# Where the first layer's sums lie, and at which steps W2's halving and the overflow's count are issued

## The chip, the cores and the metric

The kernel runs on one core of a Trainium2 chip. The metric is the time of one execution on the device, in microseconds (us). Five engines work beside one another, each with its own queue, which it takes strictly in order: TensorE (PE, with PEld for its weight loads), VectorE (DVE), ScalarE (ACT), GpSimd (POOL) and SyncE (SP), which here only issues transfers. [...]

## The reference

Attention with a decay, and behind it a layer of eight experts, of which each token uses one. Only the second part matters here. For a token with expert e:

```
logits = x @ w_gate                      # 8 experts
e = argmax(logits), or the expert of the token before it, where a local gate says so
p = softmax(logits)
h = max(x @ w1[e], 0)                    # 512 -> 1024
out = p[e] * (h @ w2[e])                 # 1024 -> 512
```

There are 8 x 576 tokens; all inputs and the output are float32.

## The kernel before

**Precision.** Every float32 operand of a matmul is cut into an upper half (float16) and a lower half (float16, what the upper one leaves out), and each product is made of three: upper with upper, lower with upper, upper with lower. An upper half is written by ScalarE (a copy to float16, L2118, for W2's blocks), a lower one by VectorE, which subtracts the upper half from the scaled value (L2120). A lower half reads two operands: the float32 block and the upper half.

**Stages.** Up to some 458 us the kernel does the attention and the routing. Then come experts 0 and 1 ("fixed", with a part of their tokens done earlier), and from 508 us on the other six, taken by the number of their tokens ("ranks" 0 to 5, with 608, 592, 576, 576, 544 and 480 places). After them stands a loop for tokens that overflow these places; the overflow's count tells how often it runs.

**A fixed expert** (`experts`): the first layer, 8 column blocks of 12 products with 256 or 320 columns into PSUM tiles `z` (two buffers, L1763), each followed by ScalarE's relu (upper half `hh`, L1737) and VectorE's lower half `hl` (L1738). Then the second layer, token tile by token tile, 24 products of 512 columns each into PSUM tiles `y` (two buffers, L1805), which ScalarE scales into SBUF (L1748) and GpSimd scatters to the output (L1750).

**A ranked expert**: the first layer goes through `seven`, which makes a 2 x 2 block product with seven products instead of eight, in 4 groups `g`. A product is 6 matmuls (L1848) of n columns, n being half the rank's places (304, 296, 288, 288, 272, 240). The seven products go into three banks: product 2 into `yt` (G.a); 1, 6, 7 and 4 accumulate in `zb` (G.b); 5 and 3 accumulate in `zd` (G.d). In between, ScalarE copies the state of `zb` to SBUF after products 1, 6 and 7 (`kept`, L1855, tiles `et`). After products 2, 7 and 3, VectorE adds a kept copy to the bank of PSUM (L1861); the sum goes to another tile `et` in SBUF. `finish` then makes `hh` of the sum by ScalarE (L1865) and `hl` by VectorE (L1866), which reads the sum and `hh`. After product 4 there is no add, and `hh` and `hl` read `zb` itself. `finish` of a sum is issued one product later. Product 3 accumulates on `zd` after the add of product 7 has read it.

The order of the products is 1, 2, 4, 6, 3, 5, 7, where 4 and 3 belong to the group before; the last group goes 1, 2, 4, 6, 5, 7, 3 and then its own 4 and 3. Each product is a step; there are 28 in the first layer, numbers 0 to 27. In the last group, steps 19 to 27, product 6 is step 22, 5 is 23, 7 is 24, the other group's 3 is 25, then 4 (26) and 3 (27). The second layer adds some 20 steps. With 592 or 608 places, the second of its token tiles is the one with the rest of the tokens; in rank 5 that tile is the first.

**Work beside the products.** The rest of the work is a list of pairs (step, function): `run` issues a function after the given step's instructions, to the queues of its engines. A step is thus a place in the queues, not a time. In each rank, beside the products:

- `M.second(j, c, low)`: the halves of the rank's own W2, in blocks j = 0 to 3, c = 0 or 1. Block 0 is cut in the rank before (step `UB`), blocks 1 to 3 here at the steps of `UC`: a pair (upper, lower) for each of the six half blocks.
- `N.load`: SP's transfers of the next rank's weights, 512 KB each, into buffers `stg`. Four are issued at step 0, three at the steps of `UN`, and each of those three takes the buffer that a block of `M` has left.
- `XA`: at step 4, GpSimd's gathers of the next rank's tokens (L1695); at step 20, SP's transposes of them (L1700).
- `LA`: at steps 6 to 13, eight operations of GpSimd (`sums`, L2132, L2136, L2141 twice, for c = 0 and 1): sums and differences of the next rank's W1 blocks, 512 columns each, all in SBUF.
- From step 28 on, the token sums (`sums_of`) and the halves of W1 of the next rank (L2098).

Rank 5 has no next rank, so only `M.second` is left there. In fixed expert 0 GpSimd's sums for rank 0 are issued at steps 9 to 16 (`FA`), and `OV[1]`, the overflow's count (`tiles`, from L2409 on, nine small VectorE operations and a memset), at step 13. Its first layer has 16 steps, 0 to 15.

Of the kernel before, what the change touches and what calls it, by code (L numbers as in the profile page):

```python
# [10 lines left out]
F32 = mybir.dt.float32  # L11
# [87 lines left out]
SEVEN = (1, 1, 1, 1, 1, 1)  # L99
WP = (28, 30, 32, 36)  # L100
LA = (6, 7, 8, 9), (10, 11, 12, 13)
UC = (0, 1), (2, 3), (8, 10), (15, 17), (22, 23), (26, 27)
UB = 45
UN = (5, 18, 28)
XA = (4, 20)
WC = (28, 29, 29, 30, 31, 31, 38, 38)
TA = (28, 36, 37, 44)
# [9 lines left out]
def kernel(  # L117
# [14 lines left out]
    DM = H * D  # L132
# [1696 lines left out]
    def seven(W, xT, sums, n, hh, hl):  # L1829

        (bh, bl, ah, al), (th, tl) = W[0:4], sums
        half = slice(0, n), slice(n, 2 * n)

        def given(d, h):
            return lambda c: (xT[:, 2 * d + c, half[h]], xT[:, 4 + 2 * d + c, half[h]])

        def summed(d, h):
            return lambda c: (th[:, c, d, half[h]], tl[:, c, d, half[h]])

        prods = {1: (ah[:, 0], al[:, 0], given(0, 0)), 2: (bh[:, 0], bl[:, 0], given(1, 0)), 3: (bh[:, 2], bl[:, 2], given(1, 1)),  # L1840
                 4: (bh[:, 1], bl[:, 1], summed(1, 0)), 5: (ah[:, 1], al[:, 1], summed(0, 0)),
                 6: (ah[:, 2], al[:, 2], summed(1, 1)), 7: (bh[:, 3], bl[:, 3], summed(0, 1))}

        def mul(p, g, out, start):
            hi, lo, x = prods[p]
            ops = [(w[:, c, g * 128:(g + 1) * 128], v) for c in range(2) for w, v in zip((hi, hi, lo), (*x(c), x(c)[0]))]
            for i, (w, v) in enumerate(ops):
                nc.tensor.matmul(out, lhsT=w, rhs=v, start=(start and i == 0), stop=(i == len(ops) - 1), skip_group_check=True)  # L1848

        def temp():  # L1850
            return EX["fx"].tile([128, 304], F32, name="et", bufs=5)[:, 0:n]

        def kept(x):
            t = temp()
            nc.scalar.copy(t, x)  # L1855
            return t

        def out(fc, h, x, plus=None):
            if plus is not None:
                t = temp()  # L1860
                nc.vector.tensor_tensor(t, x, plus, ALU.add)  # L1861
                x = t

            def finish():
                nc.scalar.activation(hh[:, fc, half[h]], x, AF.Relu)  # L1865
                nc.vector.scalar_tensor_tensor(hl[:, fc, half[h]], x, 0.0, hh[:, fc, half[h]], ALU.max, ALU.subtract)  # L1866

            if plus is None:
                finish()
            else:  # L1870
                later.append(finish)

        later = []

        def do(p, G):
            if p == 1:
                G.b, G.d = (products(1).tile([128, 512], F32, name=x)[:, 0:n] for x in ("zb", "zd"))
            if p == 2:
                G.a = ps3_.tile([128, DM], F32, name="yt")[:, 0:n]
            bank_of = G.a if p == 2 else G.d if p in (3, 5) else G.b  # L1880
            mul(p, G.g, bank_of, p in (1, 2, 5))
            if p in (1, 6, 7):
                G.kept[p] = kept(G.b)
            if p == 2:
                out(G.g, 0, G.a, G.kept[1])
            elif p == 4:
                out(4 + G.g, 0, G.b)
            elif p == 7:
                out(4 + G.g, 1, G.d, G.kept[7])
            elif p == 3:  # L1890
                out(G.g, 1, G.d, G.kept[6])
            while len(later) > (p in (2, 3, 7)):
                later.pop(0)()

        old = None
        for g in range(4):
            G = types.SimpleNamespace(g=g, kept={})
            own, last = ((1, 2, 4, 6, 5, 7, 3), (4, 3)) if g == 3 else ((1, 2, 4, 6, 3, 5, 7), ())
            for p in own:
                x = old if p in (3, 4) else G  # L1900
                if x:
                    do(p, x)
                    yield
            old = G
        for p in last:
            do(p, old)
            if p == last[-1]:
                for f in later:
                    f()
            yield  # L1910
# [104 lines left out]
    ps2_ = ctx.enter_context(tc.tile_pool(name="ps2_", bufs=2, space=PSUM, side="right"))  # L2015
# [3 lines left out]
    def products(kind):  # L2019
        if PZ.get("kind") != kind:  # L2020
            if PZ:
                PZ["stack"].close()
            PZ["kind"], PZ["stack"] = kind, ExitStack()
            PZ["pool"] = PZ["stack"].enter_context(tc.tile_pool(name="psz%d" % len(PZ), bufs=2, space=PSUM))
        return PZ["pool"]
# [180 lines left out]
    def both(*fs):  # L2206
        return lambda: [whole(f) for f in fs]
# [4 lines left out]
    todo = [turn_xl, both(last[0]), both(last[1]), both(*last[2:], close_attention, crit[0]), both(crit[1]), both(crit[2]), both(*crit[3:6]), both(*crit[6:8]), both(*crit[8:10]),  # L2212
            both(*crit[10:13]), both(*crit[13:16]), both(crit[16]), both(*crit[17:19], all_idx, late_tok)]
# [269 lines left out]
    OV = overflow()  # L2483
# [18 lines left out]
    def call(x, f, *args):  # L2502
        return x, lambda: f(*args)
# [7 lines left out]
    def tokens_of(r):  # L2511
        xn = xp_.tile([128, 8, 608], F16, name="xT")
        return xn, *token_steps(xp_, xn, lambda i: T.ranki[:, 0, r, i:i + 1], RANKC[r], bufs=XG)

    N = EX["N"]
    todo = [(8, half_rows), (13, OV[1])]
    todo += [(x, f) for x, f in zip(FA[0], [f for c in C2 for f in N.sums(c)])]
    todo += [(FA[1][0], lambda: N.room(True))]
    todo += [call(FA[1][2 * i + c], f, c) for i, f in enumerate((N.second_row, N.differences)) for c in C2]
# [6 lines left out]
    todo = [call(FA[2][2 * i + c], f, c) for i, f in enumerate((N.first_row, N.total)) for c in C2]  # L2526
# [3 lines left out]
    for r in range(NR):  # L2530
        M, xc, todo = N, xn, []
        todo += [call(y, M.second, (i + 2) // 2, i % 2, low) for i, x in enumerate(UC) for low, y in enumerate(x)]
        if r + 1 < NR:
            N = Halves(lambda r=r: number(r + 1))
            N.x = None
            xn, gs, ts = tokens_of(r + 1)
            todo += [call(0, N.load, ST)] + [call(x, N.load) for x in UN]
            todo += [(XA[0], both(*gs)), (XA[1], both(*ts))]
# [10 lines left out]
        if not SEVEN[r]:  # L2549
            todo = [(x - 12 if x > 27 else x * 16 // 28, f) for x, f in todo]  # L2550
# [89 lines left out]
```

## Time and profile before

| what | us |
|---|---|
| median of 3 runs | 794.24 (793.62 to 799.51) |
| the profiled execution | 788.54 |
| its span | 786.6 |
| TensorE busy | 736.1 (94%) |
| VectorE busy | 613.7 (78%) |
| ScalarE busy | 509.9 (65%) |
| GpSimd busy | 474.8 (60%) |

Rows of the timeline give start, duration, engine, line, operation, out<-in, shape and count; a bracket holds the idle time of the engine ahead of the row and what ended it. TensorE's matmuls are pipelined: a row lasts longer than the distance to the next one's start. The mean granted clock of TensorE over the span is 0.989.

### The profile page before, as it was taken

The numbers are of one execution on the slowest core, as the hardware profiler recorded it, in microseconds if no ns is written. First come the engines' busy times: TensorE is split into PE (matmuls) and PEld (weight loads), VectorE is DVE, ScalarE is ACT, GpSimd is POOL, SyncE is SP. The second block draws the span as 40 slices with busy tenths as digits, with TensorE's granted clock in tenths as the row PEclk, the third lists the DMA queues.
The fourth block names the chain that finished last, engine by engine and source line by source line (L and its number), as shares of the span: only waits on it lengthen the run. The fifth ranks groups of instructions, "written<-read, shape, count | busy, mean of one in ns | idle before, by whom it ended". The sixth has DMA issues, their size and how long they took to land.

```text
span 786.6 us, 21919 instructions
## 1 busy us (share of the span) xinstructions
PE 736.1 (94%) x8661; PEld 535.4 (68%) x8661; DVE 613.7 (78%) x1295; ACT 509.9 (65%) x1006; POOL 474.8 (60%) x521
## 2 busy tenths in 40 slices
PE   5898999999999998989799989999999999998996
PEld 3686888887878877878555565675665657475682
DVE  7786888898898989899758865678687896878650
ACT  7796788988878978868533225456564555657451
POOL 5879969395879859838682474191552838264201
PEclk9999999999999999999999999999999999999999
DMA  7569869788786968155794746274753716664201
GB/s 177 134 129 208 179 151 184 171 147 208 148 193 129 179 146 154 38 108 187 177 266 163 231 115 153 71 242 82 261 124 143 216 67 242 134 234 114 82 2 50
DMA packets 189659, 120.75 MB, mean 154 GB/s; under 512 B 129397, under 2 KB 165511, under 8 KB 189532
## 3 DMA queue, kind: packets, MB, share of 16 engines
q1 hardware_dynamic: 183473, 100.19, 54.1%
q0 software_dynamic: 6080, 19.13, 7.2%
q8 instruction: 69, 1.13, 0.6%
q14 instruction: 37, 0.30, 0.1%
HBM read 72.25 MB, written 19.32 MB: 116 GB/s over the span
## 4 chain that ended last, share of the span: by engine, by line
PE 54%; DVE 15%; issue 12%; POOL 8%; ACT 7%; POOLq 2%; DMA 0%; SPq 0%; ACTq 0%; DVEq 0%
PE y L1805 15%; PE pt L940 8%; PE st L894 6%; PE z L1763 6%; PE xp L919 5%; PE zb L1848 4%; DVE nm L905 3%; DVE pl L949 3%; PE st L429 2%; POOLq L1749 2%; ACT ph L945 2%; ACT P L925 2%; PE zd L1848 2%; DVE hl L1866 1%; POOL s L2141 1%
## 5 line engine op out<-in xcount | busy, mean ns | idle before, releaser
L925 ACT ACTIVATE P<-st,nm 128x512 f32<-128x512 f32 (+3 forms) x288 | 153.0, 588 | 28.0 <-DVE nm L905 23.4
L945 ACT CAST ph<-pt 128x512 f16<-128x512 f32 (+1 forms) x200 | 115.4, 588 | 35.8 <-PE pt L940 33.5
L905 DVE TENSOR_REDUCE nm<-st 128x1 f32<-128x512 f32 (+4 forms) x264 | 133.4, 542 | 6.4 <-PE st L901 3.9
L949 DVE TENSOR_TENSOR pl<-pt,ph 128x512 f16<-128x512 f32 (+1 forms) x165 | 109.2, 670 | 22.9 <-ACT ph L945 20.9
L940 PE MATMUL pt<-ident,P 128*128 128x128 f32 x784 | 121.3, 280 | 5.0 <-DVE pl L949 2.4
L1750 POOL DMA_INDIRECT out_dram<-o,ranki x26 | 34.4, 1323 | 134.7 <-ACT o L1748 102.6
L940 PEld LDWEIGHTS pt<-ident,P 128*128 128x128 f32 x784 | 84.1, 142 | 21.6 <-DVE pl L949 3.7
L919 PE MATMUL xp<-VH,pl 128*128 128x65 f16 (+1 forms) x960 | 89.2, 194 | 6.0 <-DVE pl L949 5.3
L919 PE MATMUL xp<-VH,ph 128*128 128x65 f16 (+1 forms) x960 | 90.6, 195 | 2.0 <-ACT ph L945 2.0
L1805 PEld LDWEIGHTS <-hh 128*128 128x128 f16 x528 | 51.3, 98 | 58.5
L919 PE MATMUL xp<-VL,ph 128*128 128x65 f16 (+1 forms) x960 | 90.1, 194 | 0.0
L919 PEld LDWEIGHTS <-ph 128*128 128x128 f16 (+1 forms) x1920 | 82.9, 102 | 10.3 <-issue 3.0
L894 PE MATMUL st<-Ak,Aq 128*128 128x256 f16 (+4 forms) x448 | 77.7, 284 | 4.6 <-ACT P L925 2.6
L919 PEld LDWEIGHTS <-pl 128*128 128x128 f16 (+1 forms) x960 | 74.7, 102 | 7.2 <-DVE pl L949 6.3
L894 PE MATMUL st<-KB,QB 70*128 70x256 f16 (+4 forms) x448 | 77.4, 281 | 1.9 <-DMA KB<-Ak 1.9
L1805 PE MATMUL y<-uh,hh 128*128 128x512 f16 x168 | 63.7, 379 | 0.0
L1805 PE MATMUL y<-ul,hh 128*128 128x512 f16 x168 | 63.7, 379 | 0.0
L1805 PE MATMUL y<-uh,hl 128*128 128x512 f16 x168 | 63.7, 379 | 0.0
L1763 PE MATMUL z<-xT,wh 128*128 128x384 f16 (+2 forms) x256 | 55.1, 306 | 3.4 <-DVE hl L1738 3.2
L1866 DVE SCALAR_TENSOR_TENSOR hl<-et,hh 128x288 f16<-128x288 f32 (+4 forms) x72 | 40.0, 555 | 23.3 <-ACT hh L1865 21.6
L1865 ACT ACTIVATE hh<-et 128x288 f16<-128x288 f32 (+4 forms) x72 | 31.4, 436 | 30.0 <-DVE et L1861 29.7
L1848 PEld LDWEIGHTS <-wh 128*128 128x128 f16 x384 | 37.5, 98 | 18.2 <-issue 9.8
(436 smaller groups left out, 2000.9 us busy)
## 6 DMA issues: line engine op xcount, KB each, us to landing
stg<-in_moe_w_dram SPq DMA_DIRECT2D x64, 512.0 KB
xs<-xr SPq DMA_DIRECT2D x16, 512.0 KB
ldq<-in_q_dram SPq DMA_DIRECT2D x14, 512.0 KB
ldk<-in_k_dram SPq DMA_DIRECT2D x14, 512.0 KB
ldv<-in_v_dram SPq DMA_DIRECT2D x28, 256.0 KB
QB<-Aq SPq DMA_DIRECT2D x15, 256.0 KB
KB<-Ak SPq DMA_DIRECT2D x15, 256.0 KB
ldv<-in_v_dram SPq DMA_DIRECT2D x20, 64.0 KB
```

The source lines that it names most:

```text
L894: nc.tensor.matmul(st[p0:p0 + m, co:co + n], lhsT=queries(lq, kk, h, c), rhs=rhs, start=(ps == 0 and first and co == col), stop=(ps == 1), ...
L905: nc.vector.tensor_reduce(dst, src, axis=AX.X, op=ALU.max, negate=True)
L919: nc.tensor.matmul(xo, lhsT=a[:, c0:c0 + m], rhs=w[:, vi, :], start=False, stop=(i == n - 1 and jj == 2), skip_group_check=True)
L925: nc.scalar.activation(P[:, c0:c1].rearrange("p (k x r) -> p k r x", r=2, x=64), st[:, c0:c1].rearrange("p (k r x) -> p k r x", r=2, x=64) ...
L940: nc.tensor.matmul(U["pt"][:, i * 128:(i + 1) * 128], lhsT=P[:, i * 128:(i + 1) * 128], rhs=ident, is_transpose=True, start=(i == 0), stop ...
L945: nc.scalar.copy(U["ph"][:, :cols], U["pt"][:, :cols])
L949: nc.vector.tensor_tensor(U["pl"][:, :cols], U["pt"][:, :cols], U["ph"][:, :cols], ALU.subtract)
L1750: nc.gpsimd.indirect_dma_start(out=outf if EX.get("over") else next_out(), out_offset=bass.IndirectOffsetOnAxis(ap=scat(t)[0:m], axis=0), ...
L1763: nc.tensor.matmul(z[:, a, 0:wd], lhsT=w[:, d, fc * 128:(fc + 1) * 128], rhs=xT[:, x, a * wd:(a + 1) * wd], start=(i == 0), stop=(i == len ...
L1805: nc.tensor.matmul(y[0:m], lhsT=a[:, fc, t * 128:t * 128 + m], rhs=u[:, fc], start=(i == 0), stop=(i == len(prods) - 1))
L1848: nc.tensor.matmul(out, lhsT=w, rhs=v, start=(start and i == 0), stop=(i == len(ops) - 1), skip_group_check=True)
L1866: nc.vector.scalar_tensor_tensor(hl[:, fc, half[h]], x, 0.0, hh[:, fc, half[h]], ALU.max, ALU.subtract)
```

## The change

The sum of a kept copy and a PSUM bank (`out`) is written in place into that bank, and after product 7, whose bank `zd` is still to be accumulated on, into a new PSUM tile `y` of the second layer's pool. `UC` and `UN` put the halving of W2's blocks 2 and 3 and two of the three loads at other steps. The overflow's count goes from step 13 to step 19 of fixed expert 0, which is in its second layer.

```diff
-UC = (0, 1), (2, 3), (8, 10), (15, 17), (22, 23), (26, 27)
+UC = (0, 1), (2, 3), (4, 5), (22, 23), (24, 25), (26, 27)
 UB = 45
-UN = (5, 18, 28)
+UN = (5, 24, 29)
...
-        def out(fc, h, x, plus=None):
+        def out(fc, h, x, plus=None, more=False):
             if plus is not None:
-                t = temp()
+                t = ps2_.tile([128, DM], F32, name="y")[:, 0:n] if more else x
                 nc.vector.tensor_tensor(t, x, plus, ALU.add)
                 x = t
...
             elif p == 7:
-                out(4 + G.g, 1, G.d, G.kept[7])
+                out(4 + G.g, 1, G.d, G.kept[7], True)
...
-    todo = [(8, half_rows), (13, OV[1])]
+    todo = [(8, half_rows), (19, OV[1])]
```

## Rows read from the trace of the kernel before

**Rows 1.** The page, busy time of TensorE: us (share of the span) xinstructions.
```profile
PE 736.1 (94%) x8661; PEld 535.4 (68%) x8661; DVE 613.7 (78%) x1295; ACT 509.9 (65%) x1006; POOL 474.8 (60%) x521
```

**Rows 2.** Waits of PE, 508 to 760 us: us in total, times, longest.
```profile
PE zb L1848 <- ACT et L1855: 7.8, 7, 1.6
PE zd L1848 <- DVE et L1861: 0.2, 1, 0.2
```

**Rows 3.** Busy time by windows: first layers of ranks 0, 4, 5; second of 1.
```profile
core 0: us, PE busy (x) PEld busy (x) DVE busy (x) ACT busy (x) POOL busy (x), PEclk, DMA share, GB/s
...
508.30:531.40 23.10, 22.12 (x171) 16.50 (x170) 16.68 (x30) 13.69 (x33) 19.63 (x15) 1.00 0.77 252
...
579.20:603.70 24.50, 24.50 (x198) 13.23 (x196) 20.86 (x26) 14.07 (x20) 7.18 (x5) 1.00 0.34 74
...
696.10:718.50 22.40, 19.98 (x171) 16.45 (x170) 16.56 (x30) 12.92 (x33) 17.12 (x13) 1.00 0.73 247
...
742.00:759.80 17.80, 17.80 (x182) 16.91 (x181) 12.77 (x31) 13.02 (x34) 0.93 (x1) 1.00 0.05 15
```

**Rows 4.** Timeline of rank 0's first layer, 519 to 529 us: start, us, engine.
```profile
519.17 1.28 POOL L2132 TENSOR_TENSOR stg<-stg 128x512 f32<-128x512 f32 x1
...
519.41 1.38 DVE L1866 SCALAR_TENSOR_TENSOR hl<-et,hh 128x304 f16<-128x304 f32 x1 [0.60 <-ACT hh L1865]
...
523.64 1.76 DVE L2120 SCALAR_TENSOR_TENSOR wl<-stg,wh 128x512 f16<-128x512 f32 x1
...
526.68 0.29 PE L1848 MATMUL zd<-tl,uh 128*128 128x304 f16 x1
...
526.81 0.29 PE L1848 MATMUL zd<-th,ul 128*128 128x304 f16 x1
...
527.64 0.39 ACT L1855 COPY et<-zb 128x304 f32<-128x304 f32 x1
...
527.93 0.63 ACT L2118 ACTIVATE wh<-stg 128x512 f16<-128x512 f32 x1
...
528.09 0.29 PE L1848 MATMUL zb<-th,wh 128*128 128x304 f16 x1 [0.98 <-ACT et L1855]
```

**Rows 5.** Lines L1866 and L1861: form, count, ns min/median/max, first and last start.
```profile
L1866 DVE SCALAR_TENSOR_TENSOR hl<-et,hh x72: 400/467/1491, 511.7 to 760.8; 128x288 f16<-128x288 f32 x24, 128x304 f16<-128x304 f32 x12, 128x296 f16<-128x296 f32 x12, 128x272 f16<-128x272 f32 x12
L1866 DVE SCALAR_TENSOR_TENSOR hl<-zb,hh x24: 407/446/474, 515.2 to 759.3; 128x288 f16<-128x288 f32 x8, 128x304 f16<-128x304 f32 x4, 128x296 f16<-128x296 f32 x4, 128x272 f16<-128x272 f32 x4
...
L1861 DVE TENSOR_TENSOR et<-zd,et x48: 399/445/475, 512.9 to 759.9; 128x288 f32<-128x288 f32 x16, 128x304 f32<-128x304 f32 x8, 128x296 f32<-128x296 f32 x8, 128x272 f32<-128x272 f32 x8
```

**Rows 6.** Timeline of rank 5, VectorE, and TensorE's first tile of its second layer.
```profile
757.32 0.69 DVE L2120 SCALAR_TENSOR_TENSOR ul<-stg,uh 128x512 f16<-128x512 f32 x1 [0.39 <-ACT uh L2118]
...
760.81 0.41 DVE L1866 SCALAR_TENSOR_TENSOR hl<-et,hh 128x240 f16<-128x240 f32 x1 [0.47 <-ACT hh L1865]
...
761.27 0.33 PE L1800 MATMUL y<-hl,uh 128*128 128x96 f16 x4
```

**Rows 7.** Timeline of fixed expert 0, 465 to 484 us, VectorE, GpSimd and TensorE.
```profile
465.65 1.20 DVE L2410 TENSOR_SCALAR nov<-nov 128x8 f32<-128x8 f32 x1
...
469.68 0.75 DVE L1738 SCALAR_TENSOR_TENSOR hl<-z,hh 128x256 f16<-128x256 f32 x2
...
483.68 1.23 DVE L2098 SCALAR_TENSOR_TENSOR ul<-stg,uh 128x1024 f16<-128x1024 f32 x1 [5.98 <-ACT uh L2097]
...
466.78 1.27 POOL L2132 TENSOR_TENSOR stg<-stg 128x512 f32<-128x512 f32 x1
...
469.48 2.51 POOL L2141 TENSOR_TENSOR s<-stg,s 128x512 f32<-128x512 f32 x2
...
470.14 0.27 PE L1763 MATMUL z<-xT,wh 128*128 128x256 f16 x1 [2.25 <-DVE hl L1738]
```

**Rows 8.** Timeline of VectorE behind rank 0's first layer, and at rank 1's start.
```profile
536.16 1.39 DVE L1920 TENSOR_TENSOR sx<-xT 128x1184 f32<-128x1184 f16 x1 [1.96 <-DMA xT<-xg]
...
558.22 0.47 DVE L1861 TENSOR_TENSOR et<-yt,et 128x296 f32<-128x296 f32 x1 [3.78 <-PE yt L1848]
```

## The prediction

> **What bounds the kernel now.** I read the page first: TensorE is busy 94% of the span [rows 1], so only its idle time can be won, and I looked for that in the part that the change touches: from fixed expert 0 (458 us) to the first layer of the last ranked expert (760 us). The table by windows shows where it is. The first layers of ranks 0 and 4 have TensorE idle for 1.0 and 2.4 us; that of rank 5, the only one beside which GpSimd makes no weight sums, has none (17.80 busy of 17.80) [rows 3]. The second layers have none either (24.50 of 24.50 in one, and likewise in the others). The list of waits says for what: 7.8 us in 7 waits for the copy of zb (ScalarE, L1855) and 0.2 in one for an add [rows 2].
>
> These numbers are a little short. Inside a stream two matmuls of 304 columns start 0.13 us apart while each row lasts 0.29, so the idle time of each stop is counted 0.16 us short [rows 4]. With 8 stops the loss is 8.0 + 8 x 0.16 = 9.3 us.
>
> Why the copy is late is in the timeline of rank 0 [rows 4]. GpSimd starts its first sum at 519.17. VectorE's hl (L1866) of 519.41 takes 1.38 us and the W2 lower half (L2120) of 523.64 takes 1.76, where the line view has medians of 0.467 for hl, and an L2120 with GpSimd idle takes 0.69 [rows 5, 6]. VectorE falls behind, ScalarE stands behind VectorE's add in its own queue, its copy starts only at 527.64, and TensorE starts product 7 of the last group at 528.09 after 0.98 us of idling.
>
> The line view shows which instructions GpSimd holds up. hl with x in SBUF (et) spreads from 0.400 to 1.491; hl with x in PSUM (zb) never exceeds 0.474, and the adds, with one operand in PSUM, never 0.475 [rows 5]. Both live through the same sums. So what is held up has two operands in SBUF; one with an operand in PSUM is not.
>
> Fixed expert 0 has the same trouble in another form. The overflow's count is issued at step 13, inside sums; its small `nov` operation over 8 columns takes 1.20 us, the hl behind it comes at 469.68, and TensorE waits for it until 470.14, 2.25 us, the larger of 2 such waits [rows 7].
>
> **The change part by part.**
>
> *Sums in PSUM.* 12 adds per rank, 72 in all, write PSUM instead of SBUF, and the 72 relu and 72 hl behind them read PSUM. No instruction is added or removed. By the rows above, hl then has one SBUF operand and costs 0.446 instead of 0.467 alone, and is not held up by sums. Thus the cause of the 1.38 us row is gone. What an add costs that writes PSUM no row shows. From below: 0 extra, as hl and the adds read PSUM at no extra cost. From above: the part of an add that doesn't depend on columns once more. Adds run from 0.399 (240 columns) to 0.475 (304) [rows 5], 1.2 ns a column, which leaves 0.11 us. I take 0, by the nearest rows (the same adds); 0.11 would put some 0.2 us on rank 5 and 0.1 on each other rank, 0.7 us in all.
>
> [...]
>
> Banks held longer: product 2's bank (yt) until its hl, but it is written next 7 steps later; product 7's y tile, 2 buffers over 4 groups; zd until its own hl, next written two groups later. At the end of the layer the second layer's first y tile takes the buffer of group 2, whose hl ended some five steps before, the second that of group 3, needed only a tile (24 matmuls of 512 columns) later. I cost these at 0; the cover is whole steps of 0.78 us (6 x 0.13).
>
> *W2's halving.* Block 2 moves from steps 8, 10, 15, 17 to 4, 5, 22, 23, block 3 from 22, 23, 26, 27 to 24 to 27: three lower halves (L2120) now lie at 23, 25, 27 where two lay at 23 and 27. The steps are places in the queues, not times. Where are the sums really? They start at 519.17 in rank 0 and a set of four, undisturbed, takes 471.99 - 466.78 = 5.2 us [rows 7], so two sets end at 529.6; the layer, without stops, ends at 508.3 + 28 x 0.776 = 530.0. So the sums run beside steps 14 to 27 and the three lower halves still meet them. What this costs: the first lower half can start about 1.15 us after step 22 ends (copy 0.39, upper half 0.63 [rows 4], and some start-up), takes 0.69, then comes product 7's add, 0.45, which must have read zd before product 3 writes it at step 27, 4 x 0.776 = 3.1 us after step 22's end. That leaves some 0.75 us at 304 columns, and, scaling the step by columns, 0.45 at 272. A lower half that meets a sum was held up by 1.76 - 0.69 = 1.07 us at most in rows 4, by the rest of one sum of 1.28. If it comes at a random place in it, the mean of what exceeds 0.45 to 0.75 is 0.1 to 0.3 us a rank: 0.8 us over ranks 0 to 4, with bounds of 0 and 5 x 0.6 = 3.0. The old stop, of the copy at step 24, goes: no lower half lies between steps 5 and 23 any more and hl isn't held up, so add, relu and copy of steps 20 to 22 are on time, as rank 5 shows, which had lower halves at 8 to 17, no sums, and no stop.
>
> Rank 5 has no sums but loses a little: its second layer begins with the tile that needs product 3 of the last group, and TensorE waits at 761.27 already for the hl of 760.81 to 761.22 [rows 6]. VectorE has no idle time between steps 25 and 26, so one more lower half there (0.69) puts off the last add, relu and hl: 0.5 to 0.7 us, I take 0.6.
>
> The lower half at step 5 meets the gathers on GpSimd, as that at step 10 did: 0.
>
> *Loads.* The two moved loads on SP's queue (18 to 24, 28 to 29) feed blocks of the next rank, over 20 us later: 0. The step-20 transposes stood behind the step-18 load and that behind a lower half of step 17; now they stand before it, and VectorE's wait for xT after the layer (1.96 us in rank 0 [rows 8]) shrinks. It is not on TensorE's path: 0, but it pays for VectorE's later finish.
>
> *Overflow's count.* From step 13 to 19 of fixed expert 0, in the second layer, where TensorE needs nothing of VectorE. VectorE has 5.98 us of idle time ahead of 483.68 [rows 7], and the count's small operations, 4.0 us as held up here (465.65 to 469.68), fit in. TensorE gets back 2.25 + 0.16 = 2.4 us [rows 7]. Bounds 1.8 and 2.4.
>
> **The sum.** -9.3 - 2.4 + 0.8 + 0.6 = -10.3 us, on an execution of 788.5: 778.2. The runs' median is 794.24, 5.7 above the profiled execution; I carry that over: 784.0.
>
> **The rivals.**
>
> 1. *The halving collides at the end of the layer.* The sums run until 529.6, so all three lower halves are held up by nearly a whole sum, in every rank; the add of product 7 is late at step 27 (up to 0.6 us), and the last lower half late for the last eighth of the first tile of the second layer (VectorE's queue then ends some 4 us after the layer; the tile needs that block 22 matmuls of 512 columns, or 22 x 0.22 = 4.8 us, after, so up to 0.5 more). 5 x 1.1 + 1.2 in rank 5 = 6.7 lost of 11.7: saves 5, 789. For: sums' times. Against: one held-up row of 1.07 is the worst seen, and a sum's rest is shorter on average.
> 2. *The stop moves to the next rank.* VectorE ends later, the weights and token sums of the next rank come late, and its products wait. VectorE has 3.78 us idle at the start of rank 1 [rows 8], so only a delay beyond that counts; with 1.5 us a rank in 5 ranks given back: 791.
> 3. *It does not do what it says*: the sums hold up VectorE for another reason than operands (writes of hl to SBUF, for instance), and only the count's 2.4 us is won: 792. Against: hl from zb writes the same tile and was not held up.
> 4. *Slower.* A lower half placed at 23, 25 or 27 is held up by sum after sum, not by one. Product 3 at step 27 then waits what exceeds some 0.6 us. The gain is eaten when that reaches (11.7 - 0.6)/5 = 2.2 us a rank, that is when a lower half waits 2.8 us, two sums and more; with four sums (5.2) it is 4.6 a rank, 23 - 11.1 = 12 slower: 806. Against: in rows 4 the lower half went in after one sum.
>
> **How the numbers follow.** Forecast 0.62, rival 1 0.22, rival 2 0.06, rival 3 0.05, rival 4 0.05. The forecast alone runs from 782.5 (all 11.7 us) to 787 (bounds of 3.0 and 1.2 for the two losses). Runs of the kernel before lie between 793.6 and 799.5, and the profiled one at 788.5, so runs at that level would give 778; with rivals 1 and 2 at 789 and 791, the range is 778 to 792. About 1%, 8 us, is what a measurement of this kernel can tell from no change: faster takes the forecast and a little of rival 1, 0.63; within 1% rivals 1 to 3, 0.32; slower 0.05.
>
> **What would show it.** Right: the spread of hl from PSUM ends below 0.5 us; no wait of TensorE for the copy L1855 over 0.3 us; the wait of 2.3 us in fixed expert 0 gone, `nov` after the last hl of the first layer. The lower halves of steps 23 to 27 still at 1 us and over in ranks 0 to 4, with small waits of zd at step 27. Rank 5: a wait of about 0.7 us at the third eighth of its first tile. Wrong: hl still over 1 us (rival 3); waits of more than 1 us at zd or at the second layer's start (rivals 1 and 4); TensorE waiting for weights at the start of a rank (rival 2).

## The result, and the profile after

The changed kernel takes 784.44 us (median, 781.43 to 785.3), the kernel before 794.89 beside it: a ratio of 0.985 [0.980, 0.990], 10.5 us less. The prediction was 784.0. One run of e9 below (796.88 us), slow by over 1.5% against the fastest of its kernel, is left out of its median and ratio.

The answer to [rows 1] is one line of the page after, of an execution of 785.3 us with a span of 783.6. VectorE is busy 19.5 us less, GpSimd 8.6 less; TensorE does the same work.

```profile
PE 736.3 (94%) x8661; PEld 535.6 (68%) x8661; DVE 594.2 (76%) x1295; ACT 507.5 (65%) x1006; POOL 466.2 (59%) x521
```

The line views of hl (L1866) and the add (L1861) answer [rows 5]: form, count, ns min/median/max, first and last start.

```profile
L1866 DVE SCALAR_TENSOR_TENSOR hl<-yt,hh x24: 396/457/475, 509.4 to 752.8; 128x288 f16<-128x288 f32 x8, 128x304 f16<-128x304 f32 x4, 128x296 f16<-128x296 f32 x4, 128x272 f16<-128x272 f32 x4
L1866 DVE SCALAR_TENSOR_TENSOR hl<-y,hh x24: 408/458/477, 511.8 to 755.2; 128x288 f16<-128x288 f32 x8, 128x304 f16<-128x304 f32 x4, 128x296 f16<-128x296 f32 x4, 128x272 f16<-128x272 f32 x4
...
L1861 DVE TENSOR_TENSOR yt<-yt,et x24: 406/458/483, 507.9 to 751.8; 128x288 f32<-128x288 f32 x8, 128x304 f32<-128x304 f32 x4, 128x296 f32<-128x296 f32 x4, 128x272 f32<-128x272 f32 x4
L1861 DVE TENSOR_TENSOR y<-zd,et x24: 409/467/483, 510.6 to 754.3; 128x288 f32<-128x288 f32 x8, 128x304 f32<-128x304 f32 x4, 128x296 f32<-128x296 f32 x4, 128x272 f32<-128x272 f32 x4
L1861 DVE TENSOR_TENSOR zd<-zd,et x24: 405/456/475, 514.1 to 756.7; 128x288 f32<-128x288 f32 x8, 128x304 f32<-128x304 f32 x4, 128x296 f32<-128x296 f32 x4, 128x272 f32<-128x272 f32 x4
```

No hl is held up any more: the longest takes 0.477 us, where one took 1.491. An add that writes PSUM takes 0.456 to 0.467 in the median, against 0.445 and 0.451 to SBUF.

In fixed expert 0 the count now runs behind the first layer, and hl keeps its pace (VectorE; the answer to [rows 7]).

```profile
468.50 0.42 DVE L1738 SCALAR_TENSOR_TENSOR hl<-z,hh 128x256 f16<-128x256 f32 x1 [0.89 <-ACT hh L1737]
469.81 0.42 DVE L1738 SCALAR_TENSOR_TENSOR hl<-z,hh 128x256 f16<-128x256 f32 x1 [0.89 <-ACT hh L1737]
...
475.21 0.17 DVE L2410 TENSOR_SCALAR nov<-nov 128x8 f32<-128x8 f32 x1
```

`nov` takes 0.17 us instead of 1.20. But the waits of TensorE in the ranks, which answer [rows 2], look as if half of the trouble had stayed. These are those of the change's first profile, from 506 to 757 us (total, times, longest):

```profile
PE zb L1848 <- ACT et L1855: 4.8, 5, 2.7
PE zb L1848 <- issue: 0.6, 1, 0.6
```

and these are those of the same kernel on another chip (the run `e8_whole_third` below), from 500 to 744 us:

```profile
PE zd L1848 <- DVE y L1861: 0.2, 1, 0.2
```

The first layers, timed from the first product to the first matmul of the second layer, show both (us):

| | before | change, first profile | change, e8 |
|---|---|---|---|
| fixed expert 0 | 13.53 | 10.48 | 11.12 |
| rank 0 | 22.87 | 22.07 | 21.71 |
| rank 1 | 22.62 | 25.70 | 21.14 |
| rank 2 | 22.36 | 22.44 | 20.58 |
| rank 3 | 22.94 | 20.99 | 20.99 |
| rank 4 | 22.37 | 20.54 | 19.58 |
| rank 5 | 17.32 | 17.28 | 17.28 |
| the six ranks | 130.48 | 129.02 | 121.28 |

What the first profile lost in its ranks, 129.02 - 121.28 = 7.7 us, does not come with the change alone: the same kernel lacks it in e1 and e8, and the last section shows what it looks like. The profile of e8 shows what the change does: 9.2 us less in the ranks, 2.4 in fixed expert 0. Its whole span is 16.0 shorter than that of before, but 5.0 of these lie ahead of 458 us, where nothing was changed. The windows of ranks 0, 4 and 5 in e8 (duration, then busy time and instructions of each engine) answer [rows 3]: TensorE is busy through all of them, and VectorE's work in rank 0 falls from 16.48 us (508.33 to 531.20; the 16.68 of [rows 3] is of a slightly longer stretch) to 13.79.

```profile
500.91:522.62 21.71, 21.71 (x170) 16.41 (x169) 13.79 (x29) 13.31 (x33) 18.08 (x15) 1.00 0.92 273
682.28:701.86 19.58, 19.58 (x171) 16.44 (x169) 12.73 (x28) 12.39 (x33) 15.48 (x13) 1.00 0.98 260
725.40:742.68 17.28, 17.28 (x170) 16.45 (x169) 11.54 (x29) 11.85 (x33) 0.93 (x1) 1.00 0.04 15
```

### The profile page after: what moved, and what is told of

Read it like the earlier page. It is cut to its first block, busy times and chain, and to the rows that moved or that the text cites. A ratio compares the mean times of both kernels' runs of the same rounds, so it can differ in the third digit from the quotient of the medians.

```text
span 783.6 us, 21920 instructions
## 1 busy us (share of the span) xinstructions
PE 736.3 (94%) x8661; PEld 535.6 (68%) x8661; DVE 594.2 (76%) x1295; ACT 507.5 (65%) x1006; POOL 466.2 (59%) x521
## 4 chain that ended last, share of the span: by engine, by line
PE 61%; DVE 13%; issue 10%; ACT 7%; POOL 4%; DMA 2%; POOLq 1%; another core or an unknown queue 1%; SPq 0%; ACTq 0%; DVEq 0%
PE y L1805 16%; PE pt L940 8%; PE st L894 7%; PE zb L1848 6%; PE xp L919 6%; PE z L1763 5%; DVE nm L905 4%; DVE pl L949 3%; PE zd L1848 3%; PE st L429 3%; ACT ph L945 2%; ACT P L925 2%; DMA KB<-Ak 2%; POOLq L1749 1%; PE yt L1848 1%
## 5 line engine op out<-in xcount | busy, mean ns | idle before, releaser
L945 ACT CAST ph<-pt 128x512 f16<-128x512 f32 (+1 forms) x200 | 115.1, 587 | 37.9 <-PE pt L940 34.2
L940 PE MATMUL pt<-ident,P 128*128 128x128 f32 x784 | 120.8, 279 | 6.0 <-DVE pl L949 3.4
L940 PEld LDWEIGHTS pt<-ident,P 128*128 128x128 f32 x784 | 83.5, 141 | 22.9 <-DVE pl L949 5.2
L1805 PEld LDWEIGHTS <-hl 128*128 128x128 f16 x264 | 25.8, 98 | 30.7
L1855 ACT COPY et<-zb 128x288 f32<-128x288 f32 (+4 forms) x72 | 28.1, 392 | 25.7 <-PE zb L1848 18.4
```

The costliest lines, as they stand in the source:

```text
L940: nc.tensor.matmul(U["pt"][:, i * 128:(i + 1) * 128], lhsT=P[:, i * 128:(i + 1) * 128], rhs=ident, is_transpose=True, start=(i == 0), stop ...
L945: nc.scalar.copy(U["ph"][:, :cols], U["pt"][:, :cols])
L1805: nc.tensor.matmul(y[0:m], lhsT=a[:, fc, t * 128:t * 128 + m], rhs=u[:, fc], start=(i == 0), stop=(i == len(prods) - 1))
```

## The experiments

Theory: GpSimd's sums hold up VectorE's operations with two operands in SBUF; the change takes hl out of their reach, and moves the lower halves and the count out of their way. Rivals: something else holds VectorE up; or one of the parts does nothing.

### The whole again, and its parts one by one

The first four ran on one chip. `e1_whole_again` is the change unaltered.

> The whole change once more, for a second profile. Theory (two SBUF operands are held up by GpSimd's sums): the first layers of ranks 0 to 4 take what their matmuls take (28 products: 21.7, 21.2, 20.6, 20.6, 19.5 us) with under 0.5 us of waiting each, fixed expert 0's first layer 10.5 to 11.1 us, rank 5 a wait of 0.5 to 0.7 at its first tile; about 10 to 11 us faster than before. In the first profile of the change, ranks 0, 1, 2 and 4 had further waits of 0.4 to 2.9 us, at places where PE's rows ended 0.4 to 3.7 us ahead of the semaphore that they raise. If these belong to the change (rival: VectorE's writes into PSUM disturb PE), they come back at the same places; if they belong to that execution, they lie elsewhere or are gone.

Measured: 775.75 us (772.99 to 777.17) against 787.02, ratio 0.986 [0.983, 0.989]. First layers 11.13 and 121.34 in sum, as in e8. No wait for the copy is left in the ranks, one of 0.22 for an add in rank 3.

`e2_psum_only` keeps the old steps, that of the count too:

```diff
-                t = temp()
+                t = ps2_.tile([128, DM], F32, name="y")[:, 0:n] if more else x
```

> Only the sums into PSUM; W2's halving and the count where they were. Theory: hl never above 0.5 us, so the waits for the copy fall from 9.3 us to 0 to 2 (the lower halves of steps 17 and 23 still meet the sums, 1.07 us each at most, and VectorE has room for one of them); 7 to 9 us faster. Rival (the steps do it): less than 3 us.

Measured: 781.43 us, ratio 0.992 [0.989, 0.995]; the six first layers take 123.07, 7.4 less than before. hl is at most 0.475, but lower halves at the old steps still meet sums (up to 1.87), and three waits for the copy are left, 1.6 us in total:

```profile
PE zb L1848 <- ACT et L1855: 1.6, 3, 0.9
```

`e3_steps_only` keeps the sums in SBUF:

```diff
-UC = (0, 1), (2, 3), (8, 10), (15, 17), (22, 23), (26, 27)
+UC = (0, 1), (2, 3), (4, 5), (22, 23), (24, 25), (26, 27)
-UN = (5, 18, 28)
+UN = (5, 24, 29)
```

> Only W2's halving and the two loads at the new steps. Theory: hl with et still rises to 1.3 us and more beside the sums, but the held-up lower half of step 17 (1.75 us) is gone from ahead of the copy, so the waits fall from 9.3 to 3 to 6 us, and new ones come for zd at step 27; rank 5 loses 0.5; 2 to 6 us faster. Rival (the steps do nothing without PSUM): no change or slower by 0.5 us. Rival (the steps do it all): 8 us and more.

Measured: 780.96 us, ratio 0.993 [0.990, 0.995]; the six first layers take 123.05, again 7.4 less. This was not expected: I had 3 to 6 us of waits left. VectorE's and GpSimd's rows in rank 4 show that hl is held up as before, here by some 1.75 us, beside the sum whose row begins behind it. (At the 0.44 us that the hl of 697.87 takes, this one would have ended at 700.2, ahead of that row; how a row's start stands to the holding-up stays open.) TensorE's one wait in that layer is 0.57.

```profile
699.76 2.20 DVE L1866 SCALAR_TENSOR_TENSOR hl<-et,hh 128x272 f16<-128x272 f32 x1
...
700.36 1.29 POOL L2132 TENSOR_TENSOR stg<-stg 128x512 f32<-128x512 f32 x1
...
703.10 0.28 PE L1848 MATMUL zb<-th,wh 128*128 128x272 f16 x1 [0.57 <-ACT et L1855]
```

So either part alone takes away most of the stops: 7.4 and 7.4, but 9.2 together. In ranks 0, 1, 2 and 4 of before both stand ahead of a stop, an hl of 1.29 to 1.49 us and a lower half of some 1.75; with either gone VectorE mostly catches up before the copy is due. It is no rule that a stop needs both: in rank 3 of before no hl exceeds 0.57, and two lower halves of 2.31 and 1.76 come ahead of its stops of 0.44 and 1.44.

`e4_count_only` moves the count alone:

```diff
-    todo = [(8, half_rows), (13, OV[1])]
+    todo = [(8, half_rows), (19, OV[1])]
```

> Only the overflow's count at step 19. Theory: fixed expert 0's first layer from 13.53 to about 11.1 us, all else as before; 2.4 us faster, about 0.3%, which the timing can barely tell. Rival: the wait moves to the next operation that meets the sums, and the first layer stays above 12.5.

Measured: 783.29 us, ratio 0.9955 [0.9931, 0.998], 3.7 us less. The ranks are as before to 0.01 us each; the first layer of fixed expert 0 takes 10.48 instead of 13.53. In the profiles that leave the count at step 13 and have the sums it takes 13.5 to 15.1, with the count moved 10.5 to 11.2, so the count is worth 2.3 to 4.6 us.

### Which of the moved halves

`e5_one_half_moved` moves the halves of block 2 alone, to steps 4, 5, 8 and 10, with the sums in SBUF:

```diff
-UC = (0, 1), (2, 3), (8, 10), (15, 17), (22, 23), (26, 27)
+UC = (0, 1), (2, 3), (4, 5), (8, 10), (22, 23), (26, 27)
```

> The kernel before, with one half block of W2 (block 2, c = 1) taken from steps 15, 17 to 8, 10 and its neighbour from 8, 10 to 4, 5; steps 22 to 27 and all else as before, sums in SBUF. Theory now (the copy is late by what the hold-ups between steps 14 and 22 add up to beyond what VectorE can make good, and either the hl or the lower half of step 17 is enough to bring it back): the waits for the copy in ranks 0 to 4 fall from 9.3 us to under 2.5, as in the run with the new steps alone, and rank 5 has no wait at its first tile; the first layers sum to 122 to 123 us. Rival (it is the new places at the end that help): the first layers stay above 127.

Measured: 784.38 us in one run, against 788.52. The first layers take 126.2, which misses the 122 to 123 expected: ranks 0 to 2 are as good as in e3, ranks 3 and 4 keep five waits of 0.6 to 0.8 us. The sums come earlier in these ranks (8.9 and 7.7 us into the layer, against 10.4 and more in ranks 0 to 2), where the lower half of step 10 meets them and takes 1.75. These moves are worth 4.3 us, all those of e3 7.4.

`e6_sums_later` was to take the sums out of the first layer:

```diff
-LA = (6, 7, 8, 9), (10, 11, 12, 13)
+LA = (28, 29, 30, 31), (32, 33, 34, 35)
-WC = (28, 29, 29, 30, 31, 31, 38, 38)
+WC = (29, 34, 29, 30, 32, 36, 39, 39)
```

> The kernel before, with GpSimd's sums of ranks 1 to 5 issued at steps 28 to 35, in the second layer (and the halves that read them a little later); sums of products in SBUF, W2's halving at the old steps. Theory (GpSimd's sums hold VectorE up): hl with et falls below 0.6 us in the first layers and every L2120 in them to 0.69, TensorE's waits there are under 0.5 us, first layers of ranks 0 to 4 at 21.7, 21.2, 20.6, 20.6, 19.5; the hold-ups turn up in the second layers, at L2098 and L1920, and the next rank may wait up to 3 us for its weights. Rival (something else holds VectorE up, the gathers or transposes for instance): hl still above 1 us.

It told nothing on the cause, since the sums did not move. The first layers are the old ones (130.5 in sum; 782.97 us in one run). GpSimd's first sum in rank 0:

```profile
513.87 1.27 POOL L2132 TENSOR_TENSOR stg<-stg 128x512 f32<-128x512 f32 x1
```

The layer begins at 503.03 there, so the sum starts 10.84 us into it; before, 519.17 - 508.33 = 10.84 [rows 4]. A step is a place in a queue, and nothing on GpSimd's queue ahead of the sums waits for the second layer.

`e7_halves_early` is the change with all lower halves put ahead of step 16 and `half_rows` at step 19:

```diff
-UC = (0, 1), (2, 3), (4, 5), (22, 23), (24, 25), (26, 27)
+UC = (0, 1), (2, 3), (5, 6), (8, 9), (11, 12), (14, 15)
-UN = (5, 24, 29)
+UN = (5, 18, 28)
-    todo = [(8, half_rows), (19, OV[1])]
+    todo = [(19, half_rows), (19, OV[1])]
```

> The whole change, but W2's six half blocks at steps 0, 2, 5, 8, 11, 14 (lower halves one step later), ahead of where the sums run, the loads at their old steps, and the half rows of the overflow's count (a small VectorE operation at step 8 of fixed expert 0, 0.6 us of waiting in some executions) at step 19 too. Theory: rank 5's wait at its first tile (0.5) gone, no wait of zd in rank 3 (0.4), fixed expert 0's first layer 10.5; 1 to 1.5 us faster than the whole change, 0.2%, so 0.984 to 0.985 of before, which the timing can't tell from the whole change. Rival (the early lower halves make VectorE late in groups 0 to 2): waits for the copy of over 0.5 us in ranks 4 and 5, no gain or a loss of 1 us.

Measured: 778.04 us, ratio 0.9875 [0.9831, 0.9919] against 788.52; the change on the same chip (e8) has 773.61, so this is slower, as the rival had it, and not faster. The first layers take 126.3, 5 more than with the change. In rank 4 three lower halves meet the sums one after another, and the copy behind the first two makes TensorE wait 1.36 us though no hl is held up (VectorE, then GpSimd, then TensorE):

```profile
695.09 1.87 DVE L2120 SCALAR_TENSOR_TENSOR wl<-stg,wh 128x512 f16<-128x512 f32 x1
...
698.48 1.49 DVE L2120 SCALAR_TENSOR_TENSOR wl<-stg,wh 128x512 f16<-128x512 f32 x1
...
695.12 1.28 POOL L2132 TENSOR_TENSOR stg<-stg 128x512 f32<-128x512 f32 x1
...
698.16 2.94 POOL L2141 TENSOR_TENSOR s<-stg,s 128x512 f32<-128x512 f32 x2
...
701.61 0.28 PE L1848 MATMUL zb<-th,wh 128*128 128x272 f16 x1 [1.36 <-ACT et L1855]
```

So the place of the lower halves matters with the sums in PSUM too. With `half_rows` at step 19 the first layer of fixed expert 0 takes 10.48, where e8 has 11.12; the change's first profile has 10.48 with `half_rows` at step 8.

`e8_whole_third` is the change again, beside these.

> The whole change a third time, to be compared with the run above on the same chip, and as a third profile: first layers within 0.5 us of those of the second profile (121.3 in sum for ranks 0 to 5), no rows whose semaphore comes over 0.3 us late. If the late semaphores belong to the change they come back; 0.984 to 0.989 of before.

Measured: 773.61 us (770.9 to 776.69), ratio 0.982 [0.9775, 0.9865].

### The cause itself

`e9_no_sums` is the kernel before without GpSimd's sums:

```diff
-            return [add, subtract, lambda: less(0), lambda: less(1)]
+            self.s2[c], self.s3[c] = a[:, 0], b
+            return [lambda: None] * 4
```

> The kernel before without GpSimd's weight sums (the halves read unsummed blocks of the same size in their place, so the ranked experts' numbers are not the reference's; that part of the computation is left out). The gathers, the transposes, the loads, W2's halving and the sums of products in SBUF are as before. In the run with the sums at later steps they ran when they always had, since GpSimd's queue had nothing ahead of them to wait for; this one takes them away. Theory (the sums hold VectorE up): hl with et under 0.6 us, every L2120 beside the first layers at 0.69, count and half rows at 0.2 us an operation; first layers of ranks 0 to 4 at 21.7, 21.2, 20.6, 20.6, 19.5, of fixed expert 0 at 10.5; 12 us faster, 0.984 to 0.986. Rival (gathers or transfers hold VectorE up too): waits of over 1 us are left in the first layers and hl above 1 us.

The line views of L1866 and L2120 in it:

```profile
L1866 DVE SCALAR_TENSOR_TENSOR hl<-et,hh x72: 398/458/485, 512.2 to 760.3; 128x288 f16<-128x288 f32 x24, 128x304 f16<-128x304 f32 x12, 128x296 f16<-128x296 f32 x12, 128x272 f16<-128x272 f32 x12
L1866 DVE SCALAR_TENSOR_TENSOR hl<-zb,hh x24: 407/457/475, 516.6 to 758.8; 128x288 f16<-128x288 f32 x8, 128x304 f16<-128x304 f32 x4, 128x296 f16<-128x296 f32 x4, 128x272 f16<-128x272 f32 x4
...
L2120 DVE SCALAR_TENSOR_TENSOR wl<-stg,wh x24: 681/684/693, 505.8 to 719.9; 128x512 f16<-128x512 f32 x24
L2120 DVE SCALAR_TENSOR_TENSOR ul<-stg,uh x24: 681/684/693, 553.5 to 760.6; 128x512 f16<-128x512 f32 x24
```

With the sums gone, hl in SBUF never exceeds 0.485 and a lower half never 0.693; with them the maxima are 1.491 [rows 5] and 2.31. So the sums are what holds VectorE up. The count stands at step 13 here, and its `nov` is not held up either (VectorE; 1.20 us in [rows 7]):

```profile
467.58 0.17 DVE L2411 TENSOR_SCALAR nov<-nov 128x8 f32<-128x8 f32 x1
```

The stage times expected came in rank 3 alone (20.65; before, 22.94). The others did not: the six first layers take 129.49, that of fixed expert 0 takes 15.51 where 10.5 was expected, and the kernel 787.83 us (the median of three runs), ratio 0.989 [0.982, 0.997]. The waits, of up to 2.0 us for the copy and of 2.83 in fixed expert 0, are of the kind that the first profile of the change has, and for which VectorE is not to blame (last section): ScalarE had been idle for 2.02 us before the copy behind that of 2.0, and for 3.92 before the one in fixed expert 0. So e9 shows what holds VectorE up, and not what it is worth; that is shown by e1, e4 and e8.

### Trimming what was left

`e10_ends_trimmed` is the change with the old steps in rank 5, `half_rows` at step 19 and one other step in a fixed expert:

```diff
+UD = (0, 1), (2, 3), (8, 10), (15, 17), (22, 23), (26, 27)
-FA = (9, 10, 11, 12, 13, 14, 15, 16), (17, 18, 19, 20), (1, 4, 7, 9), (17, 22), (15, 16, 17, 18), 22
+FA = (9, 10, 11, 12, 13, 14, 15, 16), (17, 18, 19, 20), (3, 5, 7, 9), (17, 22), (15, 16, 17, 18), 22
-    todo = [(8, half_rows), (19, OV[1])]
+    todo = [(19, half_rows), (19, OV[1])]
...
+        todo += [call(y, M.second, (i + 2) // 2, i % 2, low) for i, x in enumerate(UC if r + 1 < NR else UD) for low, y in enumerate(x)]
```

> The whole change with three places trimmed: rank 5, which has no sums beside it, halves W2 at the old steps; the half rows go from step 8 to 19 of fixed expert 0; the first row's halves of fixed expert 1 go from steps 1 and 4 to 3 and 5. Theory: rank 5's wait of 0.5 us at its first tile falls to 0.1, fixed expert 0's first layer is 10.5 in place of 11.1, fixed expert 1's loses its wait of 0.3: 1.3 us less than the whole change, 0.17%, too little for the timing to tell but seen in the profile. Rival: one of the moved pieces meets something else and a new wait of over 0.3 us appears.

Measured: 782.55 us (778.73 to 788.04), ratio 0.984 [0.979, 0.989]. The change on the same chip, `e11_whole_fourth`:

> The whole change on the same chip, to stand beside the trimmed one: 0.982 to 0.988 of before; first layers of ranks 0 to 5 sum to 121.2 to 121.4 us, no late semaphores.

Measured: 783.05 us (780.85 to 791.28), ratio 0.986 [0.981, 0.992]. The first layers are not those expected: 130.77 us in sum, with late starts, and 126.52 in e10, with them too (last section). The wait in rank 5's first tile is gone in e10 (0.06 us left of 0.49), a gap of 0.29 in fixed expert 1 at which the other step aimed is still there. A gain of half a microsecond can't be told by these runs.

`e12_before_again` is the kernel before, once more:

> The kernel before once more, unchanged, for the late starts seen in the profiles of the change, of e9, e10 and e11 (ScalarE and VectorE take up a PE row's result up to 4 us after its end), which the first profile of the kernel before did not have. Theory A: they belong to the chip or the execution, and come with a median of the kernel before near 795 us; then a profile of the unchanged kernel at about 795 shows them too (behind 374 us, one of 1 us or more in the ranks' first layers, whose durations exceed the 130.5 us of the first profile by some us), and one at about 787 shows none and first layers of 130 to 131 us. Theory B: they come with the kernels that write PSUM or leave out the sums; then a profile at 795 us has none, and first layers of 130 to 131 us.

Measured: 785.48 us against 785.02, ratio 0.999 [0.996, 1.003]. The chip was one where the kernel before takes 785, and there are no late starts; the six first layers take 130.51 (130.48 in the first profile), that of fixed expert 0 takes 15.11 (13.53). So only one half of theory A was seen, and none of B's.

## Why the prediction was right, point by point

**What holds VectorE up** was read rightly, for hl and the lower halves, from the spread of hl by operand [rows 5], and e9 shows it with the sums taken away. With two operands in SBUF hl took up to 1.491 us beside the sums (2.20 in e3), with one 0.477 at most; in e9, without the sums, it took 0.485 at most with two. The prediction's own sentence, that what is held up has two operands in SBUF, was too narrow: `nov` in [rows 7] reads one tensor, from SBUF, and is held up too (1.20 us with the sums, 0.17 without). What sets it apart from hl with one operand in SBUF, no run here shows.

**The stops of 9.3 us** are gone in e1 and e8: the six first layers are 9.2 us shorter, with 0.2 of new waits among them. The correction of 0.16 us for each stop, which the idle column does not hold, was needed: the idle times alone were 8.0.

**Reading PSUM, taken as no dearer than reading SBUF:** right. The 0.446 against 0.467 of [rows 5] was read as a gain, though; with the sums gone (e9) hl takes 0.457 from PSUM and 0.458 from SBUF, so there is none.

**Writing PSUM, taken as 0:** adds to PSUM are 7 to 22 ns longer in the median than those to SBUF were, at the low end of the bounds (0 to 0.11 us). In e9 adds to SBUF take 0.451 and 0.454, so a part of this is not PSUM's. ScalarE's relu gives it back: 0.411 to 0.416 from PSUM, against 0.442 from SBUF.

**The lower halves at steps 23, 25, 27, taken as 0.8 us:** the mechanism is there as foretold, its size was 0.2 to 0.4. In rank 3 of e8 a sum holds a lower half up, product 7's add is late behind it, and product 3 waits (GpSimd, VectorE, TensorE):

```profile
654.51 2.50 POOL L2141 TENSOR_TENSOR s<-stg,s 128x512 f32<-128x512 f32 x2
...
655.87 1.69 DVE L2120 SCALAR_TENSOR_TENSOR ul<-stg,uh 128x512 f16<-128x512 f32 x1 [0.49 <-ACT uh L2118]
657.48 0.45 DVE L1861 TENSOR_TENSOR y<-zd,et 128x288 f32<-128x288 f32 x1
...
657.99 0.41 PE L1848 MATMUL zd<-xT,wh 128*128 128x288 f16 x2 [0.23 <-DVE y L1861]
```

In each of ranks 0 to 4 of e8 one or two lower halves take 0.9 to 1.69 us, but only that one reaches TensorE. The working let the sums last as long as before. They are themselves shorter in e8: L2141's median falls from 1.474 to 1.271 us, and in rank 0 they end at 522.14, 0.5 us ahead of the layer (0.1 before), so that of the three lower halves only the first, at 519.98, still meets one (1.03 us). That fits that rival 1 did not come either.

One sentence of the prediction was too bold: that 1.07 us is the worst seen. It holds for [rows 4]; in rank 3 the trace of before has a lower half of 2.31 us, held up by 1.62, which the prediction left out. By that row rival 4 was likelier than it was held to be. It did not come since in the runs of the change none exceeded 1.69.

**Rank 5, taken as 0.6 us:** 0.49 in e8 and in the first profile. There (the answer to [rows 6]) TensorE waits at the fourth group of the tile's matmuls, not the third as written, and for the upper half, not for hl; the idle column has 0.32:

```profile
757.57 0.41 DVE L1866 SCALAR_TENSOR_TENSOR hl<-zd,hh 128x240 f16<-128x240 f32 x1 [0.44 <-ACT hh L1865]
...
757.59 0.33 PE L1800 MATMUL y<-hh,uh 128*128 128x96 f16 x4 [0.32 <-ACT hh L1865]
```

**The loads and the transposes, taken as 0:** right. VectorE starts on the next tokens behind rank 0's layer without waiting, and is done earlier: at rank 1's start it now idles 5.69 us (the answer to [rows 8]).

```profile
531.14 1.39 DVE L1920 TENSOR_TENSOR sx<-xT 128x1184 f32<-128x1184 f16 x1
...
555.15 0.47 DVE L1861 TENSOR_TENSOR yt<-yt,et 128x296 f32<-128x296 f32 x1 [5.69 <-PE yt L1848]
```

**The count, taken as 2.4 us:** 2.4 in e8 and 3.05 in the first profile. The difference is `half_rows`, one of whose small operations takes 1.23 us where it meets a sum, as in e8, and 0.23 where it doesn't. The bounds of 1.8 and 2.4 were too narrow, since they came from one profile: in e12 the kernel before itself takes 15.11, 1.6 more than in that profile, with a wait of 3.3 us in place of 2.25.

**The sum:** -9.2 - 2.4 + 0.5 = -11.1 us in e8's profile, where -10.3 was worked out: the two losses were sized 1.4 and came to some 0.7.

**Carrying over 5.7 us** from the profiled execution to the median was a choice without a mechanism. It was right: beside 794.89 the change takes 784.44, beside 787.02 775.75, beside 788.52 773.61, and beside 794.94 783.05. The difference of the chips stays with the kernel. That 784.0 came so near to 784.44 is in part luck: the sum was 0.8 short by e8's profile, and the gain in medians is 10.5, 11.3, 14.9 and 11.9 us in these four comparisons. The 14.9 is more than the parts explain; the profile on that chip is e8's, 5.0 us shorter ahead of 458 us. For the same reason the median of 784 must not be compared with the profiled 788.5: the gain would seem less than half.

## What to carry to other kernels

Group the rows of one line by where their operands lie: here, of the forms of hl, only the one with two operands in SBUF spread beside GpSimd's sums, up to 1.491 us, which pointed to these, and with one operand in PSUM it stayed within 0.477; `nov`, with a single operand in SBUF, was held up all the same (1.20 us, against 0.17 without the sums). When a stop has two causes that add up to it, taking away either may give most of the gain (7.4 and 7.4, 9.2 together), so the parts' gains are not to be added. And before a stage is judged by one profile, look whether the engine that came late was itself started late.

## What was not expected of the hardware

In four profiles (the first of the change, e9, e10 and e11) ScalarE and VectorE take up what TensorE has made up to some 4 us late (3.78 in the rows below), though they idle; those of before, e1 to e8 and e12 have none of it. Rank 1 of the change's first profile, TensorE, then ScalarE:

```profile
562.31 0.29 PE L1848 MATMUL zb<-th,wl 128*128 128x296 f16 x1
...
563.82 0.29 PE L1848 MATMUL yt<-xT,wl 128*128 128x296 f16 x1
566.83 0.29 PE L1848 MATMUL zb<-th,wh 128*128 128x296 f16 x1 [2.73 <-ACT et L1855]
...
566.38 0.77 ACT L1855 COPY et<-zb 128x296 f32<-128x296 f32 x2 [4.16 <-remote]
```

The row of 562.31 is the last that the copy needs, and ends at 562.60 ("remote": the profile finds nothing on this core that ended the idle time). ScalarE has nothing ahead of the copy, idles 4.16 us and starts at 566.38, so the wait of 2.73 us looks like the old one, and has another cause. Behind it the granted clock falls from 1.00 to 0.50 for 3.4 us (the windows of the idle stretch and of the one behind it):

```profile
562.30:567.10 4.80, 2.07 (x18) 1.48 (x16) 0.70 (x2) 0.72 (x2) 4.09 (x5) 1.00 0.83 242
567.20:570.60 3.40, 3.40 (x16) 2.13 (x14) 1.86 (x5) 1.66 (x4) 3.32 (x4) 0.50 1.22 215
```

14 matmuls start 0.245 us apart there instead of 0.125, 1.7 us more. With 2.73 + 0.16 that is the 4.6 us by which this layer is longer than in e8.

It doesn't come with the change: the same kernel has it in two profiles and lacks it in two others, and it shows ahead of the changed part too (from some 375 us on: ScalarE starts the copy L945 of 378.73 after 1.02 us of idling, 0.73 after the end of TensorE's row L940 that it reads). e9, which leaves PSUM sums out, has it as well. All four lie beside medians of the kernel before of 794.9, those of e1 to e8 and e12 beside 785 to 788.5; that of before has none, and its 788.54 is none of the runs between 793.62 and 799.51. This would explain the difference of the chips, but no profile of the kernel before at 795 us was had, so that it loses as much there is not shown. What makes the starts late stays open: whether the signal came late, or the matmuls themselves, whose ends are modelled.
